# One attention step placed one pair later in VectorE's order, and another one pair sooner

## The chip, the cores and the metric

The kernel runs on one core of a Trainium2 chip. The metric is the device time of one execution in microseconds (us). The engines of a core run their own instruction streams in order and wait for one another through semaphores: TensorE (PE in the profile) multiplies matrices, PEld is its weight load, VectorE (DVE) and ScalarE (ACT) work on tiles, GpSimd (POOL) does small copies and issues some transfers, SyncE (SP) issues most transfers.

## What is computed

An attention block with 32 heads of 192 channels over 2048 queries and 2048 cached keys, and a gated feed-forward block, both on the same normalised rows.

```python
xn = _layernorm(x, axis=-1)
q = (xn @ wq).reshape(B, Sq, H, Dh) ...
scores = einsum("bhqd,bhkd->bhqk", q, k_cache) * (Dh ** -0.5)
p = _softmax(scores, axis=-1)
s = einsum("bhqk,bhkd->bhqd", p, v_cache) ... @ wo
g = _silu((_silu(xn @ w1) * (xn @ w3)) @ w2)
return x + s * g
```

x has 2048 rows of 640, w1 and w3 are 640 by 1536, and everything is bfloat16.

## The kernel before

Attention comes first, head by head (the loop at line 978), and after it the rest of the feed-forward block and the output product. Each head has four **blocks** (`qb`) of 512 queries, and each block eight **pairs** (`p`) of key tiles, 128 keys each. `step` (line 755) issues one pair: the score matmuls into a PSUM tile `st2` (line 562), the exponentials by ScalarE into a weight tile (`weights`, line 566), and value matmuls of earlier pairs (`values_quads`, line 634). A weight tile `pT2` holds two pairs, so a block uses four of them, from a pool of three buffers (line 176). The score tiles have two buffers. In pair 1 `extra` (line 1010) also issues the projection of a block of the next head's queries (`by_steps`, line 363), with two casts out of PSUM: ScalarE's into `qF`, then VectorE's into `qA` (line 386).

The value matmuls lag behind: `step` keeps up to five parts (four matmuls each, three parts to a pair) in the list `parts`, four after pair 2. So the matmuls issued after a pair's scores are two parts of the pair before the last and one of the last.

Heads 2 to 30 are "in quads" and get the sum of a row's weights from VectorE (`row_sums`, line 676). It adds weight tiles into `tree`: one half sum over pairs 0 to 3 and one over pairs 4 to 7 (`fours`, which read the weight tiles), then `join`, `fold` and `ends`, which shrink the two to a tile `e`. A transposing transfer turns `e` into `eT` (line 700). `turned_sums` (line 710) is the **normalisation**: five VectorE instructions that reduce `eT`, take reciprocals, and scale the transposed outputs `ox` into the staging tile `ostage` (lines 714, 716, 719, 722, 723). `staged` (line 580) then issues a store to `o_scr` on SyncE, after every second head. The outputs come from `evict_quads` (line 660): for each of the two output banks a copy by ScalarE (`oa`) and an addition by VectorE (`ot`, line 666), then a transposing transfer to `ox`.

What sets the order of the work around the change is a clock that counts pairs. `later(n, f)` (line 670) enters a step as due n pairs from now, and `do_chores` (line 732), called at the end of each pair, issues those that are due. `fours` is due after 2, `join`, `fold` and `ends` after 4, and `turned_sums` 6 after `ends`. That places, in VectorE's program order and for the block after next of the one that is summed: normalisation and half sum of pairs 4 to 7 at the end of pair 0; output additions and query cast in pair 1; join, fold and ends at the end of pair 2; half sum of pairs 0 to 3 at the end of pair 4. Every instruction is kept in program order on its engine (`pin`).

`do_chores` also issues one entry of `lazy` in certain pairs (`slots`). These are the steps for the next heads' exponent bounds: maxima over keys (line 419), lengths of weight columns (lines 430 to 457), and `head_bound` (line 459), which ends with an all-reduce on GpSimd (line 514). In odd heads the slot is pair 5; in even heads pairs 5 to 7 or 5 and 6.

Of the kernel before, what the change touches and what calls it, by code (L numbers as in the profile page):

```python
# [30 lines left out]
def _kernel_impl(ctx, tc, A_x, A_k_cache, A_v_cache, A_wq, A_wo, B_w1, B_w3, B_w2, out):  # L31
# [8 lines left out]
    NQB = SQ // 512  # L40
# [117 lines left out]
    def in_quads(h):  # L158
        return 1 < h < H - 1
# [14 lines left out]
    with ExitStack() as actx:  # L174
# [495 lines left out]
        def later(wait, f, *a):  # L670
            chores.append((clock[0] + wait, f, a))

        def add(out, a, b):
            pin(nc.vector.tensor_tensor(out=out, in0=a, in1=b, op=ALU.add))  # L674

        def row_sums(hd, qb, p, w):
            sm = hd["sums"]

            def fours():
                t = aq["tree"].tile([P, 2, 1024], BF16, tag="tree", name="tree")  # L680
                a, b = sm["w"]
                sm["w"] = []
                add(t[:], a[:], b[:])
                sm["t"].append(t)

            def join():
                a, b = sm["t"]
                add(a[:], a[:], b[:])
                sm["t"].pop()

            def fold():
                t = sm["t"][0]
                add(t[:, 0, :], t[:, 0, :], t[:, 1, :])

            def ends():
                t = sm["t"].pop()[:, 0, :]
                e = aq["two"].tile([P, 512], BF16, tag="e", name="e")
                add(e[:], t[:, 0:512], t[:, 512:1024])
                eT = aq["two"].tile([P, 4, P], BF16, tag="eT", name="eT")
                pin(nc.sync.dma_start_transpose(out=eT[:], in_=e[:]))  # L700
                later(6 if in_quads(hd["h"] + 1) or qb < NQB - 1 else 9, turned_sums, hd, qb, eT)

            sm["w"].append(w)
            if p % 4 == 3:
                later(2, fours)
            if p == NPAIR - 1:
                for f in (join, fold, ends):
                    later(4, f)
# [23 lines left out]
        def do_chores(h, qb, p):  # L732
            for c in [c for c in chores if c[0] <= clock[0]]:
                chores.remove(c)
                c[1](*c[2])
            slots = (5,) if h % 2 and h > 1 else (5, 6) if h > 1 and qb % 2 == 0 else (5, 6, 7)
            if p in slots and lazy and lazy[0][0] <= clock[0]:
                _, f, a = lazy.pop(0)
                f(*a)
# [15 lines left out]
        def step(hd, qb, p, extra=None):  # L755
            me = (hd["h"], qb)
            first = qb == 0 and p < 2
            st2 = scores(hd, qb, p, quads=before["quads"] if first else hd["quads"])
            old = [k for k, _ in parts if k != me]
            old_quads = bool(old) and heads_quads(old[0][0])  # L760
            if p == 1 and old_quads:
                while parts[0][0] != me:
                    next_part()
            pT2 = weights(st2, hd["nb"][qb], p)
            while late:
                late.pop(0)()
            parts.extend((values_quads if hd["quads"] else values)(hd, qb, p, pT2))
            if hd["quads"] and p % 2 == 1:
                row_sums(hd, qb, p, acc["w"])
            if p == 0:  # L770
                while sum(k != me for k, _ in parts) > (2 if old_quads else 1):
                    next_part()
            elif p == 1:
                while parts[0][0] != me:
                    next_part()
            else:
                while len(parts) > (4 + (p > 2) if hd["quads"] else 3):
                    next_part()
            if extra:
                extra()  # L780
            while late:
                late.pop(0)()
            clock[0] += 1
            do_chores(hd["h"], qb, p)
# [193 lines left out]
        for h in range(1, H):  # L978
# [10 lines left out]
            hd = heads[h]  # L989
# [11 lines left out]
            for qb in range(NQB):  # L1001
                post = []
                if (h, qb) == (H - 1, 2):
                    while chores:
                        clock[0] += 1
                        do_chores(h, qb, 2)
                    astack.close()
                    acc["hTp"] = fstack.enter_context(tc.tile_pool(name="hTp", bufs=2, side="right"))
# [401 lines left out]
```

## Time and profile before

| | before |
|---|---|
| median of 3 runs | 1919.98 us (1919.51 to 1921.93) |
| profiled execution | 1919.95 us, span 1918.4 us |
| TensorE busy | 1911.2 us |
| VectorE busy | 1426.2 us |
| ScalarE busy | 1382.2 us |
| DMA, mean over the span | 123 GB/s |

The span reaches from the first to the last instruction; the time of the execution has 1.55 us more around it. Times inside the trace count from the span's start. In a timeline a row has start, duration, engine, line, operation and tiles, and in square brackets the idle time before it and what ended that. Matmuls overlap, so the same matmuls show a longer duration in the timeline than in the chain of waits, where a piece runs from the end of the one before it to its own end.

### The profile page before, as it was taken

The page shows a single profiled execution, that of the slowest core. Times are in us where ns is not written, and L with a number is a line of the kernel's source. Part 1 is how long each engine was busy: PE and PEld are TensorE (multiplying, and loading weights), DVE is VectorE, ACT ScalarE, POOL GpSimd, SP SyncE. Part 2 cuts the span into 40 slices and gives each one's busy share as a digit, 9 for nine tenths or more (in the row PEclk, how much of TensorE's full clock was granted, in tenths as well). Part 3 has the DMA queues.
Part 4 walks back from the last instruction along what each step waited for, and adds up shares of the span by engine and source line. Part 5 has one row for each costly group of instructions (what it writes and reads, how often), then busy time and mean ns, then how long its engine had stood idle before and what let it go on. Part 6 is the DMA issues. An engine that isn't in the chain of part 4 may idle for free.

```text
span 1918.4 us, 68912 instructions
## 1 busy us (share of the span) xinstructions
PE 1911.2 (100%) x30919; PEld 1201.9 (63%) x30919; DVE 1426.2 (74%) x2558; ACT 1382.2 (72%) x1521; POOL 160.0 (8%) x308
## 2 busy tenths in 40 slices
PE   9999999999999999999999999999999999999999
PEld 5665555566666666666666666666666666454456
DVE  8658888888888888888888888888888885521111
ACT  7778888888888888888888888888888887210000
POOL 3300100000000000010000000101000000000000
PEclk9999999999999999999999999999999999999999
DMA  8735656666665656666656565656666634937673
GB/s 170 151 73 101 138 108 129 115 122 113 119 127 113 127 104 126 108 126 119 129 105 133 103 129 101 138 96 139 106 131 113 124 60 125 272 82 156 159 151 76
DMA packets 598955, 235.86 MB, mean 123 GB/s; under 512 B 523312, under 2 KB 588304, under 8 KB 598656
## 3 DMA queue, kind: packets, MB, share of 16 engines
q1 hardware_dynamic: 585712, 201.80, 54.1%
q0 software_dynamic: 8256, 24.58, 4.9%
q8 instruction: 242, 3.96, 0.9%
q10 hardware_dynamic: 4688, 5.05, 0.9%
q14 instruction: 57, 0.47, 0.1%
HBM read 54.26 MB, written 31.98 MB: 45 GB/s over the span
## 4 chain that ended last, share of the span: by engine, by line
PE 98%; DMA 0%; DVE 0%; SPq 0%; ACT 0%; POOL 0%; issue 0%
PE st L562 34%; PE obank L641 31%; PE ps L363 14%; PE ps_s L1154 8%; PE obank L621 3%; PE ps_s L1110 3%; PE ps_f L1174 2%; PE ps_gu L941 1%; PE ps_f L1190 1%; PE ps L348 0%; DMA eT<-e 0%; DMA KT<-in_A_k_cache_dram 0%; DVE tree L674 0%; SPq L116 0%; PE ps_gu L348 0%; SPq L100 0%
## 5 line engine op out<-in xcount | busy, mean ns | idle before, releaser
L570 ACT ACTIVATE pT<-st,nb 128x1024 bf16<-128x1024 f32 x1016 | 1125.2, 1113 | 188.7 <-PE st L562 152.5
L641 PE MATMUL obank<-pT,vt 64*64 64x512 bf16 x11136 | 778.4, 376 | 0.2 <-DVE ot L666 0.2
L641 PEld LDWEIGHTS <-vt 64*64 64x64 bf16 x11136 | 397.5, 107 | 221.6 <-issue 0.8
L562 PE MATMUL st<-qS,KM 64*64 64x512 bf16 (+1 forms) x1951 | 410.4, 376 | 0.4 <-POOL qS L393 0.4
L562 PE MATMUL st<-qA,KT 64*64 64x512 bf16 (+1 forms) x1951 | 410.3, 376 | 0.0
L562 PE MATMUL st<-qD,KT 64*64 64x512 bf16 (+1 forms) x1951 | 410.3, 376 | 0.0
L562 PE MATMUL st<-qA,KM 64*64 64x512 bf16 (+1 forms) x1951 | 391.3, 376 | 0.0
L562 PE MATMUL st<-qS,KT 64*64 64x512 bf16 (+1 forms) x1951 | 391.2, 376 | 0.1
L562 PE MATMUL st<-qF,KT 64*64 64x512 bf16 (+1 forms) x1951 | 391.2, 376 | 0.0
L562 PEld LDWEIGHTS <-KT 64*64 64x64 bf16 (+1 forms) x7808 | 274.9, 106 | 150.8 <-issue 0.6
L363 PE MATMUL ps<-xnT,wq 64*64 64x512 bf16 (+1 forms) x2390 | 291.1, 376 | 0.0
L363 PE MATMUL ps<-xnS,wq 64*64 64x512 bf16 (+1 forms) x2390 | 287.9, 376 | 0.0
L674 DVE TENSOR_TENSOR tree<-pT,pT 128x2048 bf16<-128x2048 bf16 x232 | 282.7, 1218 | 3.2 <-ACT pT L570 3.2
L363 PEld LDWEIGHTS <-wq 64*64 64x64 bf16 (+1 forms) x4780 | 167.4, 107 | 98.0
L674 DVE TENSOR_TENSOR tree<-tree 128x2048 bf16<-128x2048 bf16 x232 | 221.2, 954 | 4.0
L666 DVE TENSOR_TENSOR ot<-oa,obank 128x512 bf16<-128x512 f32 x232 | 148.9, 683 | 84.7 <-ACT oa L665 84.2
L562 PEld LDWEIGHTS <-KM 64*64 64x64 bf16 (+1 forms) x3904 | 144.8, 106 | 62.9 <-issue 1.2
L1154 PE MATMUL ps_s<-oT,wo_sb 128*128 128x512 bf16 x720 | 155.7, 379 | 0.0
L714 DVE TENSOR_REDUCE rs<-eT 128x4 f32<-128x512 bf16 x116 | 79.1, 681 | 60.3 <-DMA eT<-e 59.4
L1154 PEld LDWEIGHTS <-wo_sb 128*128 128x128 bf16 x720 | 70.4, 98 | 84.9 <-issue 0.2
L665 ACT COPY oa<-obank 128x512 f32<-128x512 f32 x232 | 123.6, 589 | 0.0
L386 ACT CAST qF<-ps 128x512 bf16<-128x512 f32 x123 | 72.1, 587 | 60.1 <-PE ps L363 60.1
(160 smaller groups left out, 1433.0 us busy)
## 6 DMA issues: line engine op xcount, KB each, us to landing
o_scr<-ostage SPq DMA_DIRECT2D x64, 384.0 KB, 3.4
vt<-in_A_v_cache_dram SPq DMA_DIRECT2D x62, 384.0 KB, 5.1
qS<-qA SPq DMA_DIRECT2D x240, 64.0 KB, 2.1
qD<-qF SPq DMA_DIRECT2D x120, 64.0 KB, 3.1
KM<-KT SPq DMA_DIRECT2D x60, 128.0 KB, 5.1
wo_sb<-in_A_wo_dram POOLq DMA_DIRECT2D x1, 7680.0 KB, 32.2
wq<-in_A_wq_dram POOLq DMA_DIRECT2D x31, 160.0 KB, 3.5
hT_scr<-hblk SPq DMA_DIRECT2D x16, 256.0 KB, 3.0
```

The source lines that it names most:

```text
L363: pin(nc.tensor.matmul(halves[t][c, :], lhsT=w[ROWS[t], s, c], rhs=xs[ROWS[t], s // 2, qs], start=(s == 0), stop=(s == 2 * DC - 1)))
L386: pin(c(out=dst[:, qs], in_=src))
L562: pin(nc.tensor.matmul(st2[c, t * 512:(t + 1) * 512], lhsT=k[:, c], rhs=q[ROWS[t], qs], start=(s == 0), stop=(s == 2)))
L570: pin(nc.scalar.activation(out=pT2, in_=st2[:], func=ACT.Exp, scale=SCALE, bias=nb[:]))
L621: pin(nc.tensor.matmul(acc["o"][b][:, r, (j % 2) * 256:(j % 2) * 256 + DH + 1], lhsT=pT2[ROWS[r], t * 512 + j * P:t * 512 + (j + 1) * P], ...
L641: pin(nc.tensor.matmul(acc["o"][low][ROWS[c], r, :], lhsT=vt[ROWS[r], u, p, c0:c0 + DT], rhs=pT2[ROWS[r], u * 512:(u + 1) * 512], start=(p ...
L665: pin(nc.scalar.copy(out=oa[:], in_=bank[:, 0, :]))
L666: pin(nc.vector.tensor_tensor(out=ot[:, k * 512:(k + 1) * 512], in0=oa[:], in1=bank[:, 1, :], op=ALU.add))
L674: pin(nc.vector.tensor_tensor(out=out, in0=a, in1=b, op=ALU.add))
L714: pin(nc.vector.tensor_reduce(out=rs[:], in_=eT[:], axis=AX.X, op=ALU.add))
L1110: pin(nc.tensor.matmul(ps, lhsT=oT[:, k, :], rhs=wo_sb[:, k, c0:c1], start=(k == 0), stop=(k == OC - 1)))
L1154: pin(nc.tensor.matmul(ps_of[d], lhsT=wo_sb[:, k, d * P:(d + 1) * P], rhs=part(k // KQ)[:, k % KQ, :], start=(k == 0), stop=(k == OC - 1)))
```

## The change

The normalisation is due 7 pairs after `ends` instead of 6; the value 9, for the end of the last head in quads, stays. And in odd heads the slot of the bound steps is pair 4 instead of pair 5.

```diff
-                later(6 if in_quads(hd["h"] + 1) or qb < NQB - 1 else 9, turned_sums, hd, qb, eT)
+                later(7 if in_quads(hd["h"] + 1) or qb < NQB - 1 else 9, turned_sums, hd, qb, eT)
...
-            slots = (5,) if h % 2 and h > 1 else (5, 6) if h > 1 and qb % 2 == 0 else (5, 6, 7)
+            slots = (4,) if h % 2 and h > 1 else (5, 6) if h > 1 and qb % 2 == 0 else (5, 6, 7)
```

In the order in which VectorE's instructions are issued, the five of the normalisation move from ahead of the half sum of pairs 4 to 7 to behind the query cast, ahead of join, fold and ends. Nothing else moves on VectorE, and nothing on TensorE and ScalarE. On SyncE 56 of the 64 stores to `o_scr` move behind the transposition of the outputs and the three transfers of the query tiles that follow it. On GpSimd two copies of 64 elements change places with a memset, once.

## The prediction

> **What bounds the kernel now.** I read the page first, then the waits of TensorE, then the chain of waits in order of time, and only then the timelines of VectorE, ScalarE and TensorE in two neighbouring blocks.
>
> ```profile
> span 1918.4 us, 68912 instructions
> PE 1911.2 (100%) x30919; PEld 1201.9 (63%) x30919; DVE 1426.2 (74%) x2558; ACT 1382.2 (72%) x1521; POOL 160.0 (8%) x308
> ```
>
> TensorE is busy for 1911.2 of 1918.4 us. All that any change of order can win is what TensorE still waits for. Its list of waits has five entries, and the only one inside the attention loop is this:
>
> ```profile
> PE obank L641 <- DVE ot L666: 0.2, 1, 0.2
> ```
>
> The chain in order of time shows the pace of a block (one query block of one head), and that single wait. Columns are start, duration, what.
>
> ```profile
> 764.60 2.18 PE ps L363 x40
> ...
> 771.03 5.04 DMA eT<-e
> ...
> 780.12 0.04 issue
> 780.16 1.44 PE obank L641 x20
> ...
> 790.24 2.16 PE ps L363 x40
> ...
> 1015.60 2.16 PE ps L363 x40
> ...
> 1453.74 2.16 PE ps L363 x40
> ```
>
> From 1015.60 to 1453.74 lie 35 blocks, 12.518 us each, without a hole. From 764.60 to 790.24 lie two blocks and 25.64 us instead of 25.04: 0.60 lost. There the transposed sums eT came 5.04 us after they were sent, so the normalisation stood in front of VectorE's queue and the output additions behind it were late. That is the whole prize: **0.6 us, 0.03% of the time**.
>
> The 0.60 also prices a stall. The view by stretches has it in one row (length, then busy time of PE, PEld, DVE, ACT and POOL, then TensorE's granted clock, DMA share and GB/s):
>
> ```profile
> 777.00:790.10 13.10, 12.86 (x240) 8.28 (x236) 12.00 (x20) 10.75 (x13) 0.00 (x0) 1.00 0.31 48
> ```
>
> TensorE was busy for 12.86 of 13.10 us, so idle for 0.24. In the chain an undisturbed run of the same 20 matmuls takes 1.08 us (the first row here):
>
> ```profile
> 366.82 1.08 PE obank L641 x20
> ...
> 373.51 0.65 PE obank L641 x12
> ...
> 386.03 0.65 PE obank L641 x12
> ```
>
> The disturbed one took 1.44, 0.36 more: 0.24 + 0.36 = 0.60. So a stall costs its idle time **plus 0.36**, since the chain counts overlapped matmuls from end to end and the first one after a stop shows its full length.
>
> **The change, part by part.** VectorE's time in an even head's block (start, duration, engine, line):
>
> ```profile
> 366.84 0.69 DVE L386 CAST qA<-ps 128x512 bf16<-128x512 f32 x1 [0.27 <-ACT qF L386]
> 367.45 1.94 DVE L674 TENSOR_TENSOR tree<-tree 128x2048 bf16<-128x2048 bf16 x2
> 369.43 0.42 DVE L674 TENSOR_TENSOR e<-tree 128x512 bf16<-128x512 bf16 x1
> 369.77 1.22 DVE L674 TENSOR_TENSOR tree<-pT,pT 128x2048 bf16<-128x2048 bf16 x1
> ...
> 374.56 0.69 DVE L714 TENSOR_REDUCE rs<-eT 128x4 f32<-128x512 bf16 x1 [0.57 <-DMA eT<-e]
> ...
> 376.77 1.22 DVE L674 TENSOR_TENSOR tree<-pT,pT 128x2048 bf16<-128x2048 bf16 x1
> ...
> 382.28 1.22 DVE L674 TENSOR_TENSOR tree<-pT,pT 128x2048 bf16<-128x2048 bf16 x1
> ```
>
> The five instructions of the normalisation run from 374.56 to the next start at 376.77: **2.21 us**. No work is removed or added. In the new order of VectorE they stand between the query cast (366.84) and the joining of the sums (367.45). Three consequences:
>
> 1. *Ahead of the new place.* The half sum of pairs 4 to 7 (376.77), the two output additions and the cast no longer queue behind eT. The one stall of 0.60 us goes. More there is not: the additions wait for ScalarE's copies, the cast for ScalarE's cast (0.27 here), which both hang on TensorE.
>
> 2. *Behind the new place.* Join, fold, ends and the half sum of pairs 0 to 3 (369.77; I call it A) start 2.21 us later, because the cast in front of them is tied to the projection on TensorE and does not move. Who waits for A? ScalarE: the weight tiles pT2 have three buffers and a block uses four, so the exponentials of pair 6 write the buffer that A reads. That wait is in the program now, but covered:
>
> ```profile
> 372.27 1.11 ACT L570 ACTIVATE pT<-st,nb 128x1024 bf16<-128x1024 f32 x1 [0.18 <-PE st L562]
> ...
> 383.79 2.11 ACT L570 ACTIVATE pT<-st,nb 128x1024 bf16<-128x1024 f32 x2
> ```
>
> A ends at 369.77 + 1.22 = 370.99, and pair 6 starts at 372.27, waiting for its scores: 1.28 us of cover. Behind it, TensorE first multiplies pair 6 in the group of value matmuls at 373.51. A group has three parts of four matmuls, 0.65/3 = 0.216 us each (the code keeps five parts waiting, so the group after pair 7's scores holds two parts of pair 5 and the first of pair 6); pair 6 is due at 373.51 + 0.43 = 373.94. Now 2.21 later: A ends at 373.20. A hand-over costs 0.04 (780.12 to 780.16), so the exponentials run from 373.24 to 374.35 and TensorE starts at 374.39, not 373.94: idle 0.45, loss 0.45 + 0.36 = **0.81**. In the odd head's block after it: A ends at 382.28 + 1.22 + 2.21 = 385.71, the exponentials end at 385.75 + 1.11 = 386.86, TensorE starts at 386.90 instead of 386.03 + 0.43 = 386.46: idle 0.44, loss **0.80**. The second pair in the 383.79 row is pair 6 there, ended at 385.90 now.
>
> What is late next? Pair 7's exponentials follow pair 6 at the spacing of that row, 2.11 - 1.11 = 1.00 to 1.11, and end near 375.46. They are due one pair (0.65 of scores, 0.65 of values) after pair 6's, at 375.24; the first stall moves this to 375.24 + 0.81 = 376.05. So there is no second stall, and by the next projection ScalarE has caught up. But the stall comes back in every block, since the next cast hangs on the delayed projection: the chain projection, cast, normalisation, sums, A, pair 6, values lies wholly inside one block.
>
> How many blocks? 29 heads of four give 116 normalisations. In the new order 114 of them stand ahead of a half sum A; the last two run in the last head, which has none. Sum: 114 x 0.80 = 91.2.
>
> 3. *Transfers.* The transposition of e goes out 2.21 us later. The median time to landing, and the present issue on SyncE's queue:
>
> ```profile
> eT<-e SPq DMA_TRANSPOSE x116, 2.5
> 370.15 1.24 SPq L700 DMA_TRANSPOSE eT<-e  x1
> ```
>
> Issued at 372.36 it lands near 374.9 (377.4 with the 5.04 of the worst), and the normalisation now asks for it after the next cast, at 366.84 + 0.61 + 12.52 = 379.97: VectorE's waits for eT vanish, without price. In SyncE's queue 56 of the 64 output stores fall behind the output transposition and the three query moves, still ahead of eT, which has to wait for e anyway. The stores are read only in the last stage, and their staging tile is written again four blocks later. Key and value loads behind eT slip by 2.21 us; they have blocks to spare.
>
> *Odd heads' bound steps from pair 5 to pair 4.* On VectorE nothing stands between the two places, so its order is the same with and without this; GpSimd swaps two small copies with one memset, once. Cost nothing; what hides it is that the next head needs its bound only at pair 0. These rows (VectorE's and ScalarE's timelines, and GpSimd's all-reduce with its shortest, median and longest ns) bear on that:
>
> ```profile
> 360.03 0.15 DVE L511 TENSOR_REDUCE ns<-pr 128x1 f32<-128x2 f32 x1
> L514 POOL PARTITION_ALL_REDUCE nb<-ns x34: 382/386/728, 28.3 to 1562.8; - x34
> 387.44 2.35 ACT L570 ACTIVATE pT<-st,nb 128x1024 bf16<-128x1024 f32 x2 [0.24 <-PE st L562]
> ```
>
> In an odd head's last block the three small operations follow A: 385.71 + 0.6 (an estimate: three of 0.15 with their gaps) + 0.73 gives 387.04, before the 387.44 at which pair 0's exponentials start, which themselves move 0.8 later. Without that cover they, and the values behind them, would be late once in each of 14 odd heads.
>
> **Sum.** The profiled execution took 1919.95 us (its span and 1.55 around it), the median of the runs shown is 1919.98. 1919.95 - 0.60 + 91.2 = **2010.5 us**.
>
> Bounds of the price: the 0.36 rests on one stall. If it were all swallowed, 0.44 per block remain: 114 x 0.44 - 0.6 = 49.6, 1969.5. With hand-overs of 0.1 instead of 0.04, the loss is 0.92: 2024. I take 0.80, because the one row with a stop on this very operation gives it.
>
> **The rivals.**
>
> *The slack holds (not slower).* Pair 6 is ready at 373.38 + 0.04 and due at 373.94, so it has 0.52 us in hand, and A has 1.28 before ScalarE feels it. The point where this rival decides is a slip of A of 1.8 us: up to there TensorE has no idle time. For it: VectorE had idle time that a queue can use to catch up (0.27 and 0.57 in the rows above). Against: the 0.27 lies before the cast, which TensorE fixes, the 0.57 before a wait that comes after A, and 2.21 is more than 1.8. Time: 1919.95 - 0.6 = 1919.4.
>
> *The stall is smaller.* The start after a stop is less dear, or A gets its turn sooner: 0.44 to 0.70 per block, 1970 to 1999.
>
> *A second wait in the block.* If the normalisation in its new place still waited for eT as it does today, A would slip further. Today's bill:
>
> ```profile
> DVE rs L714 <- DMA eT<-e: 59.4, 63, 2.7
> ```
>
> 59.4 more would give 2070. Against it stand the 2.5 us by which even the worst eT is early.
>
> *The clock.* TensorE would for the first time stop every 13 us. If half the clock were lost for one pair's work (1.3 us) after each stop, 114 x 1.3 = 148 more, 2159. The one stall in the trace speaks against it: the stretch 777.00:790.10 has it, its granted clock stays at full, and by it the clock costs nothing. [...]
>
> *The change does nothing it says.* The order of issue shows it does; what it does not do is alter VectorE's order by its second half. Counted under the first rival.
>
> **How the numbers follow.** Forecast, a stall of 0.7 to 0.92 in each block: 0.73. Smaller stall: 0.12. Slack holds: 0.06. Second wait: 0.07. Clock: 0.02. The predicted time is 2010.5. The forecast's own range is 1999 to 2024; it reaches down into the smaller stall, and a little up: 1984 to 2027. By 0.2% (3.8 us), about what a measurement here can tell from no change: faster at most 0.02, since the prize is 0.6 us; same 0.05; slower 0.93.
>
> **What would show it.** Right: TensorE waits for ScalarE's pT once per block, some 0.45 us each and 51 in total, right after pair 6's exponentials, which wait for A's half sum; blocks of 13.3 us; eT gone from VectorE's waits; the output addition's 0.2 gone. Wrong: blocks of 12.52 us with pair 6 waiting for its scores as now; or idle time on TensorE elsewhere, at the banks or the scores.

## The result and the profile after

The changed kernel takes 1998.11 us (median of 5 runs, 1997.9 to 1998.24), the kernel before 1919.98. The ratio is 1.0406, 95% interval 1.0392 to 1.042: **78.1 us slower**, 4.1%. The profiled execution took 1998.24 us with a span of 1996.6, 78.2 more than before.

The page, with its line of the chain of waits by engine:

```profile
span 1996.6 us, 68932 instructions
PE 1933.0 (97%) x30919; PEld 1236.6 (62%) x30919; DVE 1429.0 (72%) x2558; ACT 1375.7 (69%) x1521; POOL 172.3 (9%) x308
...
PE 51%; DVE 35%; ACT 10%; issue 2%; DMA 1%; SPq 0%; POOL 0%; ACTq 0%; POOLq 0%
```

VectorE and ScalarE are as busy as before (1429.0 and 1375.7 us against 1426.2 and 1382.2). No work was added, and yet VectorE now makes 35% of the chain that ended last. Something that ran beside TensorE has come between its matmuls. The waits say what (us in total, times, longest):

```profile
ACT pT L570 <- DVE tree L674: 89.4, 85, 1.2
...
PE obank L641 <- ACT pT L570: 56.6, 114, 0.7
```

TensorE waits 114 times for weights, once in each block in which the normalisation stands ahead of the half sum A; ScalarE waits for that half sum (85 times; in the other 29 blocks the trace puts the same wait down to a small VectorE instruction beside it, 15 times L446 and 14 times L478). VectorE's wait for eT, 59.4 us before, is no longer among its waits. One block from the chain in order of time:

```profile
375.89 2.18 PE ps L363 x40
...
378.71 0.69 DVE qA L386
379.40 0.60 DVE rs L714
...
381.17 0.42 DVE ostage L723
381.59 1.15 DVE tree L674
...
383.91 1.15 DVE tree L674
385.06 0.02 issue
385.08 0.02 ACTq L570
385.10 0.04 issue
385.14 1.12 ACT pT L570
386.27 0.04 issue
386.31 0.41 PE obank L641 x4
...
389.09 2.18 PE ps L363 x40
```

Read it from top to bottom: projection, cast of the query, five instructions of the normalisation, join and fold, A (383.91), the exponentials of pair 6 (385.14), and four value matmuls that waited for them. Before, this same stretch of the chain held matmuls only. The next projection starts at 389.09, 13.20 us after the last; before, 12.518. Over a long stretch:

```profile
1511.93 2.18 PE ps L363 x40
```

From 389.09 to 1511.93 are 85 blocks of 13.210 us. 13.210 - 12.518 = 0.692 per block, and 114 x 0.692 - 0.6 = 78.3, which is the whole difference of the spans.

The timelines of VectorE and ScalarE show that the wait is a real one, not a label:

```profile
383.83 1.22 DVE L674 TENSOR_TENSOR tree<-pT,pT 128x2048 bf16<-128x2048 bf16 x1
```

```profile
385.14 2.12 ACT L570 ACTIVATE pT<-st,nb 128x1024 bf16<-128x1024 f32 x2 [1.19 <-DVE tree L674]
```

A ends at 383.83 + 1.22 = 385.05 and pair 6 starts 0.09 later, after 1.19 us of idle time. Before, it waited 0.18 us for its scores.

### The profile page after: what moved, and what is told of

Same layout as the page of the kernel before. It is cut to its first block, busy times and chain, and to the rows that moved or that the text cites. A ratio compares the mean times of both kernels' runs of the same rounds, so it can differ in the third digit from the quotient of the medians.

```text
span 1996.6 us, 68932 instructions
## 1 busy us (share of the span) xinstructions
PE 1933.0 (97%) x30919; PEld 1236.6 (62%) x30919; DVE 1429.0 (72%) x2558; ACT 1375.7 (69%) x1521; POOL 172.3 (9%) x308
## 4 chain that ended last, share of the span: by engine, by line
PE 51%; DVE 35%; ACT 10%; issue 2%; DMA 1%; SPq 0%; POOL 0%; ACTq 0%; POOLq 0%
DVE tree L674 16%; PE ps L363 14%; PE st L562 11%; PE obank L641 9%; PE ps_s L1154 8%; ACT pT L570 6%; DVE ostage L719 4%; DVE qA L386 4%; DVE rs L714 3%; ACT qF L386 3%; PE obank L621 3%; PE ps_s L1110 3%; DVE e L674 2%; DVE ostage L723 2%; PE ps_f L1174 2%
## 5 line engine op out<-in xcount | busy, mean ns | idle before, releaser
L641 PE MATMUL obank<-pT,vt 64*64 64x512 bf16 x11136 | 805.8, 377 | 56.6 <-ACT pT L570 56.6
L641 PEld LDWEIGHTS <-vt 64*64 64x64 bf16 x11136 | 420.9, 107 | 297.1 <-issue 91.5
L562 PE MATMUL st<-qS,KM 64*64 64x512 bf16 (+1 forms) x1951 | 415.5, 376 | 0.3 <-POOL qS L393 0.3
L562 PE MATMUL st<-qD,KT 64*64 64x512 bf16 (+1 forms) x1951 | 415.7, 376 | 0.0
L562 PE MATMUL st<-qA,KT 64*64 64x512 bf16 (+1 forms) x1951 | 415.5, 376 | 0.0
L562 PEld LDWEIGHTS <-KT 64*64 64x64 bf16 (+1 forms) x7808 | 285.3, 106 | 138.5 <-issue 0.6
L363 PEld LDWEIGHTS <-wq 64*64 64x64 bf16 (+1 forms) x4780 | 174.2, 107 | 91.1
L562 PEld LDWEIGHTS <-KM 64*64 64x64 bf16 (+1 forms) x3904 | 148.8, 106 | 49.9 <-issue 1.1
L386 DVE CAST qA<-ps 128x512 bf16<-128x512 f32 x120 | 82.9, 691 | 35.7 <-ACT qF L386 35.2
```

The source lines that it names most:

```text
L363: pin(nc.tensor.matmul(halves[t][c, :], lhsT=w[ROWS[t], s, c], rhs=xs[ROWS[t], s // 2, qs], start=(s == 0), stop=(s == 2 * DC - 1)))
L386: pin(c(out=dst[:, qs], in_=src))
L562: pin(nc.tensor.matmul(st2[c, t * 512:(t + 1) * 512], lhsT=k[:, c], rhs=q[ROWS[t], qs], start=(s == 0), stop=(s == 2)))
L641: pin(nc.tensor.matmul(acc["o"][low][ROWS[c], r, :], lhsT=vt[ROWS[r], u, p, c0:c0 + DT], rhs=pT2[ROWS[r], u * 512:(u + 1) * 512], start=(p ...
```

## The experiments

The theory: the loss is one wait, A's late end, handed on by the buffer that pair 6's exponentials overwrite. The rivals: the odd heads' slots; the new order of stores and transfers, or a late normalisation as such; VectorE's load; a price in proportion to the delay.

**One part of the change at a time.**

```diff
# e1_norm_only, against the kernel before
-                later(6 if in_quads(hd["h"] + 1) ...
+                later(7 if in_quads(hd["h"] + 1) ...
# e2_slots_only, against the kernel before
-            slots = (5,) if h % 2 and h > 1 else ...
+            slots = (4,) if h % 2 and h > 1 else ...
```

> Only the normalisation is due 7 pairs after ends; the odd heads' slot stays at pair 5. If the whole loss comes from the late half sum A (pairs 0 to 3): 1998, as the changed kernel. If the slots have a share in it, below that by that share.

> Only the odd heads' slot moves from pair 5 to pair 4. VectorE's order is the same, so 1920 within 0.6 us. If the slots matter through GpSimd's order: a difference of more than 2 us.

The normalisation alone: 1998.73 us, ratio 1.0412 (1.0396 to 1.0428). The slots alone: 1919.71 against 1919.77, ratio 1.0 (0.9991 to 1.0009). The first is the change, the second has no effect that can be measured.

**The same order with a fourth weight buffer.** This takes away what makes ScalarE wait and leaves every instruction where the change put it.

```diff
# e3_four_buffers against the changed kernel; e4_before_four: the same against the kernel before
-        pp = actx.enter_context(tc.tile_pool(name="pp", bufs=3))
+        pp = actx.enter_context(tc.tile_pool(name="pp", bufs=4))
...
-        hbp = actx.enter_context(tc.tile_pool(name="hbp", bufs=2))
+        hbp = actx.enter_context(tc.tile_pool(name="hbp", bufs=1))
...
-                e = aq["two"].tile([P, 512], BF16, tag="e", name="e")
+                e = aq["one"].tile([P, 512], BF16, tag="e", name="e")
```

> The changed kernel, its order of instructions as it is, with four buffers for the weight tiles instead of three (the room comes from a single buffer for e, pt and pa). The exponentials of pair 6 no longer write the buffer that A reads; A now gates pair 0 of the next block, which is 2.6 us later. If the loss is this one wait: 1919.4. If it comes from anything else in the new order (transfers on SyncE's queue, later sums, VectorE's load): still near 1998.

> The kernel before with the same four buffers and single buffers. Control for the run before: nothing waits for A there, so 1920 within 0.6 us. If four buffers gain something of their own, it shows here.

Both missed: 1932.91 and 1931.36 us. The control is what saved the reading: it has no change in it and was 11.6 us slower than the kernel before (1919.77 in these rounds). The distance between the two is 1.55 us, not 78; the rest has another cause. In neither trace does TensorE wait anywhere in heads 2 to 30. The control's time went in the last head:

```profile
ACT pt L536 <- DVE pa L541: 10.1, 2, 5.6
...
PE obank L621 <- ACT pT L570: 7.3, 2, 3.9
```

That head makes two tiles `pt`, the gate activations of the feed-forward block, in one pair. With a single buffer the second waits up to 5.6 us for VectorE's product of the first, and ScalarE's exponentials queue behind it; TensorE's two stops there come to 7.3 of the 11.6 us (the last section has the rest). So I took the room from elsewhere:

```diff
# e9_four_clean against the changed kernel; e10_before_four_clean: the same against the kernel before
-        pp = actx.enter_context(tc.tile_pool(name="pp", bufs=3))
+        pp = actx.enter_context(tc.tile_pool(name="pp", bufs=4))
...
-            ot = aq["two"].tile([P, 1024], BF16, tag="ot", name="ot")
+            ot = aq["one"].tile([P, 1024], BF16, tag="ot", name="ot")
...
-                e = aq["two"].tile([P, 512], BF16, tag="e", name="e")
+                e = aq["one"].tile([P, 512], BF16, tag="e", name="e")
```

> The changed kernel with four weight buffers, as in e3_four_buffers, but with the room taken from e and ot (one buffer each), which are read by a transfer right after they are written; pt and pa keep two. If the 11.6 us that both kernels with four buffers had too much came from the single pt and pa in the last head: 1919.4, within 0.6 us of the kernel before. If they came from four buffers as such: 1931 again.

> The kernel before with the same buffers as e9_four_clean. Control: 1920 if the room is free of charge, 1931 if four buffers cost something as such. The distance to e9_four_clean is what is left of the change when A's buffer is not reused: 0 to -0.6 us by my theory.

1919.24 us with the change's order, ratio to the kernel before 0.9998 (0.9989 to 1.0007); 1919.93 for the control, 1.0003 (0.9994 to 1.0012). Two rows of the chain of the kernel with the change's order:

```profile
376.83 2.16 PE ps L363 x40
...
389.35 2.16 PE ps L363 x40
```

12.52 us again, and no block that can be read off this chain is longer than 12.55. **The whole 78 us hang on the reuse of one buffer.** The stores, the transfers and VectorE's order are the changed kernel's here, and cost nothing that can be measured.

**The normalisation moved further, behind A.**

```diff
# e5_behind_a, against the kernel before
-                later(6 if in_quads(hd["h"] + 1) ...
+                later(11 if in_quads(hd["h"] + 1) ...
```

> The kernel before with the normalisation due 11 pairs after ends: it stands at the end of pair 5, behind the half sum A, so A is not moved at all and the output additions still don't queue behind eT. If A's place is what counts: 1919.2 to 1920, at best 0.6 us below the kernel before. If a normalisation that is late hurts in itself (staging, stores, transfers, the bounds behind it): 1925 or more.

1919.05 us against 1919.45, ratio 0.9997 (0.9988 to 1.0006). Five pairs later is free where one pair later costs 4%: lateness of the normalisation is no harm, its place ahead of A is. This version and e9_four_clean are without the loss. In their traces TensorE never waits for `ot`, the stall of 0.6 us that the change was to remove; but neither does it in e2_slots_only and e4_before_four, which have the old order, so that stall comes and goes, and 0.6 us is below what a measurement of this kernel can tell from no change. The gain is not shown.

**A smaller and a larger delay of A.**

```diff
# e6_split, against the changed kernel
-            low = ox[:, 4:8, 0:DT]
-            pin(nc.vector.tensor_tensor(out=low, in0=low, ...
-            pin(nc.vector.tensor_tensor(out=stage(h, qb)[:, :, o0 + P:o0 + DH], ...
-            staged(h, qb)
+            def low_part():
+                ...
+            if in_quads(h + 1) or qb < NQB - 1:
+                later(4, low_part)
+            else:
+                low_part()
# e7_twice, against the changed kernel
-            pin(nc.vector.tensor_tensor(out=stage(h, qb)[:, :, o0:o0 + P], ...
+            for _ in range(2):
+                pin(nc.vector.tensor_tensor(out=stage(h, qb)[:, :, o0:o0 + P], ...
```

> The changed kernel with only the first three of the five instructions (sum, reciprocal, first multiplication) ahead of A, and the other two at the end of pair 5. A is late by about 1.55 us instead of 2.2. By a deadline: pair 6 has 1.20 us of cover at ScalarE and 0.33 us until its matmuls are due by their starts, so 0.02 to 0.05 per block, 1919.4 + 2 to 6 = 1922 to 1926. By a price in proportion to the delay: 1920 + 78 x 1.55/2.2 = 1975.

> The changed kernel with the first multiplication of the normalisation issued twice (the same result): A is late by 0.61 to 0.71 more. By the deadline every further delay counts in full: 1998.1 + 114 x 0.61 to 0.71 = 2068 to 2079. If TensorE has slack of another kind (the stall partly overlaps something): less than 2050. If VectorE becomes the bound: more than 2079.

The split: 1922.81 us, ratio 1.0016 (1.0007 to 1.0025), 3.4 us for a delay of A of 1.53 us (in its trace A starts at 384.34, 4.46 us after the cast at 379.88, against 2.93 before). In its chain the group of value matmuls with pair 6 in it is a touch longer, 0.68 and not 0.65, and nothing else is:

```profile
377.05 2.16 PE ps L363 x40
...
385.25 0.65 PE obank L641 x12
385.90 0.65 PE st L562 x12
386.55 0.68 PE obank L641 x12
387.23 0.65 PE st L562 x12
...
389.60 2.16 PE ps L363 x40
```

The block takes 12.55 us, 0.03 more than before, and 114 x 0.03 = 3.4 (2.8 if the stall of 0.6 us is taken off). So the delay is free up to a deadline, and this kernel sits just past it. A price in proportion (1975) is out.

The repeated multiplication: 2081.23 us, ratio 1.0841 (1.0824 to 1.0857), 83 us more than the changed kernel. The two copies in its chain, and two projections:

```profile
392.25 0.70 DVE ostage L720
392.96 0.02 issue
392.98 0.69 DVE ostage L720
...
401.83 2.18 PE ps L363 x40
...
415.76 2.18 PE ps L363 x40
```

The block is 13.93 us, 0.73 above the 13.20, and 114 x 0.73 = 83. The copy costs 0.73 (392.25 to 392.98), a little more than the 0.61 to 0.71 I gave it, so the time came out above my 2068 to 2079. I had named more than 2079 as the sign that VectorE had become the bound; it had not: it is busy for 1509.4 of 2079.3 us, and the wait of TensorE that grew is the same one, for pair 6, 114 times: 139.8 us in all where it was 56.6. Past the deadline the 0.73 us more on VectorE was 0.73 us more in every block.

**Giving the value matmuls more time.**

```diff
# e8_lag, against the changed kernel
-                while len(parts) > (4 + (p > 2) if hd["quads"] else 3):
+                while len(parts) > (4 + (p > 2) + (p > 4) if hd["quads"] else 3):
```

> The changed kernel with one more part of value matmuls kept waiting from pair 5 on (six instead of five), so pair 6's first part falls into the next group of TensorE, 0.86 us later than now. If the value matmuls are the only thing that waits for pair 6: 1919.4. By my account the next wait is the scores of the next block's pair 0, which use the score tile that pair 6's exponentials read and are due 0.2 us after the present stop: some 0.47 per block remain, 1919.4 + 54 = 1973, with TensorE waiting at st instead of obank.

1998.02 us, ratio 1.0407 (1.0391 to 1.0423): not one microsecond won. TensorE's list of waits shows why:

```profile
PE st L562 <- ACT pT L570: 56.6, 114, 0.7
```

The wait moved from the value matmuls to the scores of the next block's pair 0, as expected, with the same total, which I had not expected. I had reckoned 0.47 per block because these scores came four matmuls after the old stop. But keeping one more part back takes just those four matmuls out of the way, so TensorE gets to the scores 0.216 us sooner, at the very moment of the old stop. Two consumers wait for pair 6 at nearly the same point; relieving one leaves the other.

## Why the prediction was right, and where it was off

- *The bound, and the prize of 0.6 us.* The bound is right: with the loss taken away, e5_behind_a and e9_four_clean stay within 0.4 us of the kernel before. That is too close to the noise to show the 0.6 itself.
- *What is late next.* Right, and shown by the fourth buffer: A, then ScalarE's exponentials of pair 6, then the value matmuls, once in each of 114 blocks.
- *A late by 2.21 us.* Right. From the start of the cast to that of A it was 369.77 - 366.84 = 2.93 us, and is 383.83 - 378.71 = 5.12 now: 2.19 more.
- *The idle time.* 0.45 and 0.44 us foretold, 56.6/114 = 0.50 found. Part of this is the hand-over from VectorE to ScalarE: I took 0.04, and the chain has 0.02 + 0.02 + 0.04 with a semaphore instruction on ScalarE's queue. The rest, some 0.01, is within the rounding of the rows.
- *"A stall costs its idle time plus 0.36."* **This is the term that was mis-sized.** Now a stop lengthens the four matmuls behind it to 0.41 us, where they take 0.216: 0.19, not 0.36. The 0.36 came from the one stall of the kernel before, which I took for one stop. Looked at closely it was two. The rows are VectorE's two additions, and TensorE's value matmuls in two adjoining narrow stretches (the second row of TensorE is cut out of the same 20):

```profile
779.43 1.28 DVE L666 TENSOR_TENSOR ot<-oa,obank 128x512 bf16<-128x512 f32 x2
```

```profile
780.16 0.63 PE L641 MATMUL obank<-pT,vt 64*64 64x512 bf16 x8 [0.24 <-DVE ot L666]
```

```profile
780.76 0.63 PE L641 MATMUL obank<-pT,vt 64*64 64x512 bf16 x8
```

  The first eight matmuls use the first output bank. At two parts of 0.216 they should have been followed at 780.59; the next came at 780.76, after the second addition had ended at 780.71. So 0.17 of the 0.36 was a second wait, too short to leave TensorE idle by the records. With 0.50 + 0.19 = 0.69 the sum is 1919.95 - 0.6 + 114 x 0.69 = 1998.0; with my 0.80 it was 2010.5. The two misses have opposite signs, so the sum came out nearer (0.69 for 0.80) than the term did (0.19 for 0.36). By its time the result is not in the forecast's own 1999 to 2024, but just below it, where the rival "the stall is smaller" (0.44 to 0.70 per block) had its place: the mechanism came out as forecast, the price as that rival had it, and for a reason that it gave (the start after a stop is less dear).
- *No second stall, ScalarE caught up by the next projection.* Right: behind the four matmuls of 0.41 us the chain of a block holds nothing but matmuls at their usual times up to the next projection, and of the blocks that can be read off the chain one took 13.43 us and all others 13.19 to 13.22.
- *Transfers and the odd heads' slots at no cost.* Right: e9_four_clean has the transfers' new order at 0.9998, and e2_slots_only is at 1.0.
- *The rivals.* The slack was put at 1.8 us, as the delay up to which TensorE has no idle time. The loss begins sooner: the split, with A 1.53 late, already pays 0.03 per block; the change, with A 2.19 late, pays 0.69; the repeated multiplication, with A 2.92 late (390.72 to 396.57 is 5.85), pays 1.41. The delay less the loss is 1.50, 1.50 and 1.51 us, so one slack of 1.5 us prices all three. The delay less TensorE's idle time is 1.69 us in the changed kernel and in the repeated multiplication (2.19 - 0.50, and 2.92 - 139.8/114): the loss begins 0.19 us of delay before the records show TensorE idle. No second wait at eT came. The term of the clock's rival, half the clock for one pair's work after each of the 114 stops, is shown by no run: the clock stayed at 1.00 for the span of the changed kernel, and of e7_twice, where the 114 stops are 1.2 us each.

## What to carry to other kernels

When a step is moved in an in-order queue, ask what stands behind its new place, who overwrites or reads that, and when; a wait in the other direction, of a writer for a buffer's last reader, did not show in the profile while it was covered (ScalarE's wait for `tree`, 89.4 us now, is not in the list of the kernel before at all). Price the slack before the move: here 1.5 us were free and 2.2 cost 4%. And size a stall only on a stop whose matmuls show a single wait; give every experiment that changes a buffer its control.

## What the runs showed of the hardware

In the control e4_before_four TensorE stopped twice in the last head, for 7.3 us in all, 3.9 the longer one, so 3.4 the other. The granted clock fell each time; these are the stretches around the two stops (stretches with length, busy time of PE, PEld, DVE, ACT, POOL, clock, DMA share, GB/s):

```profile
1580.00:1585.00 5.00, 3.67 (x63) 2.11 (x52) 4.93 (x8) 0.95 (x2) 0.00 (x0) 1.00 0.29 54
1585.00:1590.00 5.00, 2.91 (x28) 1.97 (x30) 3.01 (x6) 3.91 (x5) 0.00 (x0) 0.57 0.14 26
1590.00:1595.00 5.00, 5.00 (x66) 3.36 (x62) 0.00 (x0) 2.69 (x4) 0.00 (x0) 0.74 0.01 3
1595.00:1600.00 5.00, 5.00 (x72) 2.98 (x68) 2.87 (x6) 3.75 (x4) 0.00 (x0) 1.00 0.00 0
1600.00:1605.00 5.00, 2.60 (x44) 1.74 (x40) 4.81 (x11) 0.21 (x1) 0.00 (x0) 1.00 0.26 82
1605.00:1610.00 5.00, 3.52 (x34) 2.42 (x36) 2.43 (x5) 4.06 (x5) 0.00 (x0) 0.66 0.78 262
1610.00:1620.00 10.00, 10.00 (x156) 6.66 (x152) 4.57 (x10) 6.60 (x6) 0.00 (x0) 1.00 0.32 107
```

TensorE's idle time in the first two rows is 1.33 + 2.09 = 3.42 us, the shorter stop; the clock is 0.57 and 0.74 in the second and third rows and 1.00 in the fourth. The idle time in the fifth and sixth rows is 2.40 + 1.48 = 3.88 us, the longer stop; the clock is 0.66 in the sixth row and 1.00 in the last. So a single stop of 3.4 or 3.9 us cost clock, while 114 stops of 0.5 us, or of 1.2 us, cost none (granted clock 1.000 over the span of the changed kernel and of e7_twice). ScalarE's exponentials, which wait for their scores there, show the pace behind the shorter stop:

```profile
1589.24 1.11 ACT L570 ACTIVATE pT<-st,nb 128x1024 bf16<-128x1024 f32 x1 [0.69 <-PE st L562]
1591.82 1.11 ACT L570 ACTIVATE pT<-st,nb 128x1024 bf16<-128x1024 f32 x1 [1.46 <-PE st L562]
...
1594.89 1.11 ACT L570 ACTIVATE pT<-st,nb 128x1024 bf16<-128x1024 f32 x1 [0.20 <-PE st L562]
1596.21 1.12 ACT L570 ACTIVATE pT<-st,nb 128x1024 bf16<-128x1024 f32 x1 [0.20 <-PE st L562]
```

A pair took 2.58 us while the clock was low and 1.32 when it was back, so TensorE worked at about half its pace. An estimate from these figures, with half the clock wherever it was not full: 0.43 x 5/0.5 = 4.3 us of the second row were at half, so the clock fell at about 1585.7, 2.0 us into the shorter stop, and all 2.91 us of matmuls behind it in that row were slow. Of the third row 0.26 x 5/0.5 = 2.6 us were at half, and of the sixth 0.34 x 5/0.5 = 3.4 us, most of them behind the longer stop. If half of these 8.9 us is lost, 4.5 us, then with 7.3 us of idle time it makes 11.8 us, a little more than the 11.6 us that this control was slower by.
